# Four layers interleaved by superblocks, score tiles of 3 and 2 banks, TensorE in the listed order

One core of one Trainium2 chip runs the whole network. The metric is device time of one execution in microseconds (us). Two timed runs were slow, one of the kernel before beside e1 to e4 (610.69 us) and one of e8 (639.11); they stand in the medians, not in the ratios. A ratio is the mean time of one kernel's fast runs over that of the other's of the same rounds, so it is not quite the ratio of the medians that stand beside it. In the lines of the profile PE is TensorE, PEld its weight loads, DVE VectorE, ACT ScalarE, POOL GpSimd, SPq the queue from which most DMAs are issued. The granted clock (PEclk) is the share of full TensorE clock that the trace records: 1.0 is full, 0.5 half, and a mean over a stretch lies between.

## The reference

Four layers over x of 2048 rows and 512 columns: attention with a sliding window of 256 (32 heads of 16), linear attention, and both again with the same weights. Each adds to the residual.

```python
def _A_ref(x, wqkv, wo):                     # "attention" below
    q, k, v = split(x @ wqkv)                # 32 heads of 16
    scores = einsum("bhqd,bhkd->bhqk", q, k) * Dh ** -0.5
    mask = (i - j >= 0) & (i - j < 256)
    p = softmax(where(mask, scores, -1e9))
    return heads_joined(p @ v) @ wo

def _B_ref(x, wqkv, wo):                     # "the linear layer" below
    phi = lambda t: where(t > 0, t + 1, exp(t)) + 1e-6   # the "feature map"
    pq, pk = phi(q), phi(k)
    kv, z = sum_s(pk * v), sum_s(pk)         # over all 2048 rows
    o = (pq @ kv) / (pq @ z + 1e-6)
    return heads_joined(o) @ wo

x = A_x
x = x + _A_ref(_layernorm(x), A_wqkv, A_wo)
x = x + _B_ref(_layernorm(x), B_wqkv, B_wo)
x = x + _A_ref(_layernorm(x), A_wqkv, A_wo)
x = x + _B_ref(_layernorm(x), B_wqkv, B_wo)
```

(Condensed: batch 1, reshapes and transposes left out.) The sums kv and z are what limits interleaving: nothing of a linear layer's second half (numerator, denominator, output projection) can start before its last row block has been summed.

## The kernel before

The rows are treated in four *superblocks* of 512. For each, the attention layer makes q, k and v, then walks through score tiles: some small matmuls on 32 rows of the array fill a PSUM tile of three banks, ACT takes one exp over the tile, POOL zeroes what the mask forbids, and small matmuls multiply the result with v (P·V). The program lists side work (the next superblock's projections, the last one's output projection) evenly among the score tiles. A linear layer starts when the attention layer is done.

```python
psA = ctx_l.enter_context(tc.tile_pool(name="psA", bufs=2, space=PSUM))   # 2 score tiles of 3 banks
psM = ctx_l.enter_context(tc.tile_pool(name="psM", bufs=2, space=PSUM))   # all else, 1 bank each
# ...
            for gi, grp in enumerate(GROUPS):
                # ...
                for b, runs in enumerate(bins):
                    PTs.append(scores(I, grp, runs))
                    s += 1
                    if gi == 0 and b < len(lns):
                        lns[b]()                       # layernorm of the next superblock
                    if b >= 1 and steps:
                        steps.pop(0)()                 # P.V of the group before
                    while side and done < ((s - 4) * total) // (slots - 4):
                        side.pop(0)()                  # one projection
                        done += 1
# ...
        for li, lt in enumerate(layers):               # "ABAB", one after the other
            with ExitStack() as ctx_l:
                if lt == "A":
                    # ...
                    layer_A(xres, xres, wA, woA, a_idx)
                else:
                    layer_B(xres, xres, wB, woB, li == len(layers) - 1)
```

## Time and profile before

The median of the three runs timed first is 607.69 us (604.7 to 607.84); the profiled execution was a further, faster run of 602.24 us, with a span of 600.2 us. The stages, cut at the first and last exp of each attention layer:

| stage | us |
|---|---|
| head, to the first exp | 41.1 |
| first attention, four superblocks | 42.7, 43.0, 43.3, 41.1 |
| joint: linear layer, then the head of the second attention | 115.5 |
| second attention | 170.4 |
| tail: second linear layer | 103 |

One more view is TensorE's waits in the kernel before: who waited, for what, us in total, how often, and the longest.

```profile
PE O L318 <- POOL pt L308: 22.7, 35, 2.5
PE A L286 <- ACT pt L298: 14.6, 40, 0.9
PE py L490 <- DMA oT<-ob: 14.1, 13, 2.1
```

P·V (O) waits for masks, scores (A) for a score tile that ACT is still reading, and the linear layer's output projection (py) for a transposing DMA; each time 0.4 to 1.1 us on average.

### The profile page before, as it was taken

The numbers are of one execution on the slowest core, as the hardware profiler recorded it, in microseconds if no ns is written. First come the engines' busy times: TensorE is split into PE (matmuls) and PEld (weight loads), VectorE is DVE, ScalarE is ACT, GpSimd is POOL, SyncE is SP. The second block draws the span as 40 slices with busy tenths as digits, with TensorE's granted clock in tenths as the row PEclk, the third lists the DMA queues.
The fourth block names the chain that finished last, engine by engine and source line by source line (L and its number), as shares of the span: only waits on it lengthen the run. The fifth ranks groups of instructions, "written<-read, shape, count | busy, mean of one in ns | idle before, by whom it ended". The sixth has DMA issues, their size and how long they took to land. (4 is left out here: it accounts for less than half of the span.)

```text
span 600.2 us, 15126 instructions
## 1 busy us (share of the span) xinstructions
PE 460.0 (77%) x6032; PEld 250.1 (42%) x6114; DVE 332.5 (55%) x729; ACT 367.5 (61%) x373; POOL 272.1 (45%) x667
## 2 busy tenths in 40 slices
PE   0178888888878879995647788888887887899573
PEld 0133455545546534452213345554544553444231
DVE  7731546545623365777886154554562336677773
ACT  1557679799779824660025857988978892466000
POOL 9444457657556562200035435675755666320000
PEclk9996899999976678997988779899998788999787
DMA  9412115031020030211431211501302103021363
GB/s 302 127 27 60 16 37 75 2 48 30 2 64 11 3 80 10 41 31 35 72 70 36 57 19 34 78 2 42 35 2 53 24 2 76 14 44 29 74 120 92
DMA packets 83375, 29.66 MB, mean 49 GB/s; under 512 B 67936, under 2 KB 82784, under 8 KB 83296
## 3 DMA queue, kind: packets, MB, share of 16 engines
q1 hardware_dynamic: 78256, 23.88, 19.9%
q10 hardware_dynamic: 5040, 4.72, 2.6%
q8 instruction: 50, 0.82, 0.6%
q14 instruction: 29, 0.24, 0.1%
HBM read 6.29 MB, written 2.10 MB: 14 GB/s over the span
## 5 line engine op out<-in xcount | busy, mean ns | idle before, releaser
L298 ACT ACTIVATE pt<-A 128x1536 bf16<-128x1536 f32 (+1 forms) x228 | 281.0, 1321 | 52.9 <-PE A L286 46.3
L308 POOL TENSOR_SCALAR_AFFINE_SELECT pt<-pt 128x384 bf16<-128x384 bf16 (+3 forms) x456 | 184.3, 430 | 140.1 <-ACT pt L298 136.1
L318 PE MATMUL O<-vbd,pt 128*128 128x34 bf16 x2880 | 108.4, 182 | 27.7 <-POOL pt L308 22.7
L318 PEld LDWEIGHTS <-pt 128*128 128x128 bf16 x2880 | 89.8, 99 | 64.8 <-POOL pt L308 37.9
L286 PE MATMUL A<-qT,kb 32*128 32x192 bf16 (+3 forms) x1920 | 96.7, 249 | 17.1 <-ACT pt L298 14.6
L286 PEld LDWEIGHTS <-kb 32*128 32x128 bf16 x1920 | 50.1, 98 | 69.6 <-issue 64.3
L490 PE MATMUL py<-woB,oT 128*128 128x512 bf16 x124 | 39.3, 448 | 16.6 <-DMA oT<-ob 14.1
L327 DVE RECIPROCAL rall<-O 128x24 f32<-128x24 f32 (+1 forms) x48 | 13.8, 288 | 66.7 <-PE O L318 66.7
L164 POOL TENSOR_SCALAR ln_ve<-ln_mv 128x1 f32<-128x1 f32 x64 | 14.0, 225 | 69.7 <-DVE ln_mv L162 68.2
L221 PE MATMUL pq<-xnT,wA 128*128 128x512 bf16 x108 | 37.3, 432 | 9.2 <-DVE ln_stats L160 5.6
L271 PE MATMUL py<-woA,oT 128*128 128x512 bf16 x108 | 33.1, 397 | 14.1 <-DMA oT<-o_sb 12.4
L160 DVE BATCH_NORM_STATS2 ln_stats<-xres 128x6 f32<-128x512 f32 x64 | 42.5, 681 | 0.8
L235 DVE TENSOR_SCALAR kb<-pk,mask_even 128x512 bf16<-128x512 f32 x32 | 25.3, 791 | 28.6 <-PE pk L232 24.4
L232 PE MATMUL pk<-xnT,wA 128*128 128x512 bf16 x116 | 36.5, 414 | 5.0 <-ACT kb L237 2.5
L403 ACT ACTIVATE phi_e<-pkb 128x512 bf16<-128x512 f32 x32 | 19.1, 598 | 32.9 <-PE pkb L426 31.4
L166 POOL TENSOR_TENSOR ln_rstd<-ln_ve,mhalf 128x1 f32<-128x1 f32 x64 | 36.8, 582 | 4.3 <-ACT xn L178 0.4
L226 DVE CAST qT<-pq 128x512 bf16<-128x512 f32 x24 | 16.6, 691 | 33.5 <-PE pq L221 33.4
L432 PE MATMUL pvb<-wB,xnTb 128*128 128x512 bf16 x124 | 34.8, 395 | 0.2
L426 PE MATMUL pkb<-wB,xnTb 128*128 128x512 bf16 x122 | 34.0, 396 | 0.5 <-issue 0.4
L272 DVE TENSOR_TENSOR xres<-py,xres 128x512 f32<-128x512 f32 x32 | 22.0, 686 | 21.4 <-PE py L271 20.5
L245 PE MATMUL pv<-wA,xnT 128*128 128x512 bf16 x114 | 31.9, 380 | 2.2 <-ACT kb L237 0.8
L178 ACT ACTIVATE xn<-xres,ln_nmr,ln_rstd 128x512 bf16<-128x512 f32 x12 | 9.6, 827 | 37.9 <-DVE ln_nmr L176 37.9
(71 smaller groups left out, 522.0 us busy)
## 6 DMA issues: line engine op xcount, KB each, us to landing
vbd<-vst SPq DMA_DIRECT2D x128, 34.0 KB, 1.9
out_dram<-ost ACTq DMA_DIRECT2D x16, 128.0 KB, 1.9
wB<-in_B_wqkv_dram SPq DMA_DIRECT2D x1, 1536.0 KB, 11.2
xst<-in_A_x_dram SPq DMA_DIRECT2D x8, 128.0 KB, 2.6
wA<-in_A_wqkv_dram SPq DMA_DIRECT2D x2, 512.0 KB, 7.2
xst<-in_A_x_dram ACTq DMA_DIRECT2D x8, 128.0 KB, 4.0
wA<-in_A_wqkv_dram ACTq DMA_DIRECT2D x1, 512.0 KB, 4.3
woA<-in_A_wo_dram ACTq DMA_DIRECT2D x1, 512.0 KB, 8.2
```

The source lines that it names most:

```text
L160: nc.vector.bn_stats(stats[:], x_ap)
L166: nc.gpsimd.tensor_tensor(rstd[:], ve[:], mhalf[:], op=ALU.pow)
L221: nc.tensor.matmul(pq[:], lhsT=w[:, c, t * P:(t + 1) * P], rhs=xnTs[I][:, c, :], start=(c == 0), stop=(c == NCT - 1))
L232: nc.tensor.matmul(pk[:], lhsT=w[:, c, D + t * P:D + (t + 1) * P], rhs=xnTs[I][:, c, :], start=(c == 0), stop=(c == NCT - 1))
L271: nc.tensor.matmul(py[:], lhsT=oT[:, c, :], rhs=wo[:, c, :], start=(c == 0), stop=(c == NCT - 1))
L286: nc.tensor.matmul(A[:, g, r, pos:pos + n, :], lhsT=kbs[m // 8][32 * rg:32 * rg + 32, t, m % 8, :, :], rhs=qTs[I][32 * rg:32 * rg + 32, t, ...
L298: nc.scalar.activation(body[:, 0:2 * ng, 0:n, :], A[:, 0:ng, :, 0:n, :].rearrange("p g r s c -> p (g r) s c"), ACT.Exp, scale=0.25)
L308: nc.gpsimd.affine_select(out=v, in_=v, compare_op=ALU.is_ge, fill=0.0, base=1 if kind == 0 else -2, pattern=[[0, nx], [2 * s, 64]], chann ...
L318: nc.tensor.matmul(O[:, u, g, :, :], lhsT=PTs[b][:, s0:s0 + 2, :], rhs=vbd[(m // 8) % NV][:, m % 8, :, grp[g], :], start=(n == 0), stop=(n ...
L426: nc.tensor.matmul(pk[:], lhsT=xnT[:, c, u * P:(u + 1) * P], rhs=w[:, c, D:2 * D], start=(c == 0), stop=(c == NCT - 1))
L432: nc.tensor.matmul(pv[:], lhsT=xnT[:, c, u * P:(u + 1) * P], rhs=w[:, c, 2 * D:3 * D], start=(c == 0), stop=(c == NCT - 1))
L490: nc.tensor.matmul(py[:], lhsT=oT[:, c, :], rhs=wo[:, c, :], start=(c == 0), stop=(c == NCT - 1))
```

## The change

The intent: fill what attention leaves idle on TensorE and VectorE with the linear layer's work, and so take that work out of the joint and the tail. Most of a linear layer's first half (keys, values, their sums, queries) goes under the attention layer ahead of it, and half of its second half under the attention layer behind it. For that all layers share one set of pools. PSUM is divided anew: one score tile of three banks, one of two, and three single banks for everything else. Masks that come in pairs become a multiplication on VectorE. And TensorE gets its instructions in the order in which the program lists them; in the kernel before, the scheduler orders them.

```diff
-        psA = ctx_l.enter_context(tc.tile_pool(name="psA", bufs=2, space=PSUM))
-        psM = ctx_l.enter_context(tc.tile_pool(name="psM", bufs=2, space=PSUM))
+        ps3 = pool("ps3", 1, space=PSUM)
+        ps2 = pool("ps2", 1, space=PSUM)
+        psM = pool("psM", 3, space=PSUM)
+        vst = [fp.tile([P, 2, NP, VW], BF, name=f"vst{k}") for k in range(2)]   # was 3
 ...
+                        if len(ps) == 2 and y - x > 1:
+                            mt = tri[kind][:].unsqueeze(1).unsqueeze(1).to_broadcast([P, y - x, 2, 64])
+                            nc.vector.tensor_tensor(v, v, mt, op=ALU.mult)
+                            continue
 ...
+            for k, (size, units) in enumerate(phs):          # a phase is one score tile
+                scores(I, bins, size, units, where)
+                while due and due[0][0] <= k:
+                    due.pop(0)[1]()                          # P.V
+                    spent += .8
+                while items and items[0][1] <= k and (spent < total * (k + 1) / len(phs) or items[0][0] == 0):
+                    c, _, f = items.pop(0)                   # side work: (cost, first phase, what)
+                    f()
+                    spent += c
 ...
+        with tc.manual_schedule(engines={mybir.EngineType.PE}):
 ...
+                    prep = prep_items(I + 1, 5)              # q, k, v of the next superblock: from phase 5
+                    if I > 0:
+                        items += prep[:4] + outproj_items(I - 1, 0, 6) + prep[4:]
 ...
+                if I > 0:
+                    items += bkv_items(I - 1, 12) + bq_items(I - 1, 12)   # linear layer: from phase 12
```

(Cut to its core; the rest moves code, reads x without a cast, and renames.)

## The prediction

> **What bounds the kernel now.** I read the page first (busy shares, slices), then cut the trace at the first and last exp of each superblock (512 rows of an attention layer, four to a layer) and asked for busy time by stretch. The page's chain that ended last follows only the final two microseconds, so it does not name a bound.
>
> ```profile
> PE 460.0 (77%) x6032; PEld 250.1 (42%) x6114; DVE 332.5 (55%) x729; ACT 367.5 (61%) x373; POOL 272.1 (45%) x667
> PE   0178888888878879995647788888887887899573
> DVE  7731546545623365777886154554562336677773
> ACT  1557679799779824660025857988978892466000
> PEclk9996899999976678997988779899998788999787
> ```
>
> No engine is the bound for the whole span. The digits show alternation: ACT is high where VectorE is low (attention, slices 3 to 14 and 22 to 33), and ACT is near zero in slices 18 to 20 and at the end, where VectorE is high. The stages, columns being stretch, length, PE busy, PEld, DVE, ACT, POOL, granted clock, DMA share, GB/s:
>
> ```profile
> 0.00:41.10 41.10, 11.18 (x63) 5.12 (x65) 28.41 (x65) 15.19 (x24) 26.30 (x55) 1.00 0.54 166
> 41.10:83.80 42.70, 35.30 (x501) 18.97 (x510) 17.36 (x31) 31.17 (x30) 18.50 (x47) 0.84 0.16 32
> 126.80:170.10 43.30, 36.99 (x704) 21.82 (x709) 23.12 (x45) 37.15 (x30) 27.33 (x69) 1.00 0.16 29
> 170.10:211.20 41.10, 32.88 (x646) 21.31 (x649) 12.00 (x26) 37.00 (x30) 25.49 (x67) 0.66 0.10 23
> 211.20:270.00 58.80, 54.48 (x317) 26.76 (x323) 38.70 (x89) 27.62 (x47) 17.70 (x41) 0.92 0.20 41
> 270.00:326.70 56.70, 34.56 (x176) 14.45 (x178) 46.35 (x121) 8.60 (x14) 12.33 (x32) 0.85 0.30 56
> 557.00:600.20 43.20, 25.21 (x126) 11.25 (x128) 26.34 (x66) 0.00 (x0) 0.00 (x0) 0.80 0.45 99
> ```
>
> So the 600.2 us are: 41 of head, 170 of attention (four times about 42.5), 115.5 between the two attention layers (59 of the linear layer's projections and sums, near a TensorE bound, and 57 of its second half plus the next head, where VectorE leads), 170 of attention, 103 of tail. In attention ACT (37 of 43) and PE (37 of 43) are both close to full and wait for one another; VectorE is half idle there.
>
> ```profile
> L298 ACT ACTIVATE pt<-A 128x1536 bf16<-128x1536 f32 x144 | 198.7, 1488 | 21.3 <-PE A L286 17.4 <-POOL pt L308 3.8
> L298 ACT ACTIVATE pt<-A 128x1024 bf16<-128x1024 f32 x72 | 71.9, 1033 | 21.6 <-PE A L286 20.1 <-POOL pt L308 1.3
> L308 POOL TENSOR_SCALAR_AFFINE_SELECT pt<-pt 128x384 bf16<-128x384 bf16 x176 | 92.2, 540 | 60.6 <-ACT pt L298 58.8 <-PE O L318 0.8
> L308 POOL TENSOR_SCALAR_AFFINE_SELECT pt<-pt 128x192 bf16<-128x192 bf16 x128 | 43.8, 357 | 38.2 <-ACT pt L298 36.8 <-PE py L271 1.4
> L405 DVE SCALAR_TENSOR_TENSOR pks<-pkb,phi_e 128x512 bf16<-128x512 f32 x32 | 22.0, 689 | 3.0 <-DVE phi_e L404 0.5
> ```
>
> **What the Trainium skill says.** (1) "TensorE: Matmul & The Clock Gate", What's actually happening: the array falls to half clock after an idle window of about 3.4 us. The trace agrees in kind: the last superblock, with no projections beside its small matmuls, has a granted clock of 0.66 against 1.00 for the one before. (2) The same page, Step-by-step: only weight loads are pulled ahead, matmuls stay in program order. So what the program lists first blocks what follows if it waits; this trace cannot show it. (3) "VectorE: DVE Perf Modes", the perf-mode tier table: tensor_tensor runs at 2x on bf16 in SBUF, at 1x with PSUM; its fp32 add formula gives 691 ns for 512 columns, and the trace has 686 to 690. (4) "GPSIMD Engine Reference", Specifications: POOL's SBUF interfaces are shared with VectorE, with contention when VectorE has two SBUF inputs. The new mask multiplications are such; no run so far shows a price.
>
> **The change, part by part.**
>
> *Scores.* The packed tiles hold the same windows (40 per pair and superblock, 30 in the first). Counted from the two lists: score matmuls fall from 1920 to 1440 with the same columns; the P·V matmuls stay 2880. Exps become 16 of three banks and 16 of two per full superblock, against 20 and 10. Durations from the rows above: 16×1.488+16×1.033 = 40.3 us against 40.1; ACT gains nothing. PSUM goes from two 3-bank score tiles plus two others to one 3-bank, one 2-bank and three others.
>
> *Masks.* 456 selections on POOL (184 us) become 568 smaller ones plus 140 multiplications on VectorE. From the four POOL shapes (540, 416, 357, 294 ns at 384, 256, 192, 128 columns) I extrapolate 232 at 64: about 84 us per layer. The 140 on VectorE, estimated with the skill's fixed part at 2x as (192+151)/0.96 = 357 ns for the large form, are 48 us in all.
>
> *VectorE's total.* 332.5; minus casts of x (7), layernorm applications (14) and their small products (9), fewer small reciprocals and block-diagonal builds (14), vbd memset (4); plus 48 for masks, 22 for the 32 copies of v taken from ACT (690 ns), 14 for adding 32 partial sums (258 columns, estimated 0.43 us), 6 for copies no longer on ACT: about 375 to 410 us. POOL stays near 255 to 270 (48 us of layernorm applied at 0.81 replaces masks). ACT falls to about 325.
>
> *Interleaving.* Three quarters of the linear layer's first half goes under attention, and in the second attention half of the previous one's second half too. TensorE per full superblock, at full clock: 32 score tiles at about 0.23 (12 matmuls took 0.40 us, of which 0.18 latency) = 7.4; 384 P·V at 0.026 (24 took 0.77, same latency) = 10; projections (48+16+48 matmuls of 512 columns) at 0.216, the pace of the dense stretch at 240 to 270 us = 24; small ones 1: 42.5 us, and 47.5 with the second half of a linear layer. ACT: 37 of exp as measured plus 8 feature maps at 0.6 = 42. VectorE: keys 5.5, q and v 5.6, statistics 6.8, masks 6.8, P·V normalisation 4.8, residual 2.7, feature maps 8.0, v copies 2.8, sums 1.7 = 44.7, with the second half 51. All three stand at 42 to 51, where they were 37, 37 and 23.
>
> I take 90% for the fullest engine, hence 52 us for superblocks 2 and 3 of the first attention and 57 in the second; the last (no next projections: ACT 42 leads) 47; the first (ACT 31, half clock at its start) 35. Attention: 35+52+52+47 = 186, and 35+57+57+47 = 196; against 170 each.
>
> *Head.* x is loaded before the weights and read as bf16 without a cast, only four row blocks are normalised before the projections; the old kernel had 16 x-loads, all weights and 16 statistics there and projected from 30 to 41 us. Data at 5, normalised and transposed by 13, twelve projections on a partly cold array 15: 28 us, 13 less.
>
> *Between the layers.* PE is in program order here, so latencies add: P·V remainder 4.4; four transposes 6.3 (issue 1.3 each, 2.4 to landing), last projection and residual 1.6; layernorm to first transposed block 5.3; eight projections with waits for the sums 12; queries 3.5; second half of the first superblock 11 (denominator, four numerators, four transposes, projection); layernorm 9.3; next q, k, v 12 (VectorE-bound: 4×1.4+8×0.69); first score 1. Sum 66; 68 with some half clock; was 115.5.
>
> *Tail.* The first five items, 33, then four second halves at about 10, as each waits for its transposes before the next is issued: 74 with the store; was 103.
>
> Sum: 28+186+68+196+74 = 552. The runs of the old kernel lie 2 to 7 us above its profiled span, so about **555 us**.
>
> **The rivals.** *Program order stalls attention.* One matmul waiting for one of the three general PSUM banks holds all that follow, scores too. O keeps one bank nearly always; two serve some 28 projections per superblock. A feature-map bank is held about 0.95 for matmuls, 1.5 behind a running exp, 0.6, 0.3 and 0.7: 4 us. If that were every bank's hold, a superblock would need 28×4/2 = 56 us and more with VectorE's queue: superblocks of 60 to 65, total near 595. For it: ACT already lost 38 us to waits for scores with two equal tiles. Against it: copies of q and v hold a bank only about 2 us, and old attention ran well with one bank free beside O.
>
> *VectorE becomes the bound*, by the mask contention above and lumps: near 580; for it its digits rise from 23 to 45-51 in a superblock, against it POOL's load does not rise.
>
> *Overlap nearly perfect.* The dense 512-column work keeps the clock at 1.00 where it was 0.66 to 0.84, and full superblocks take 46 to 49: attention 170 and 178, mid 62, tail 65: near 508. For it: the clock row; against it: the latencies of program order.
>
> **Range and chances.** 80% from 508 to 600. Removed serial time (13+47+29 = 89 us) is surer than the price in attention (42 us). Faster by over 2% means under 595.5: 0.87; within 2%: 0.08; slower: 0.05.
>
> **What would show it.** First exp near 28 us instead of 41; superblocks of 50 to 58 with exps, feature maps and projections mixed, clock above 0.9 in the middle ones; VectorE's busy time 375 to 410; gaps of some 68 us between the last exp of one attention and the first of the next, and 74 after the last. Wrong would be: score matmuls mostly waiting for VectorE or for feature maps (first rival), a mask multiplication far above 360 ns (second), or a gap of 90 us and more between attentions, which would mean program order exposes latencies that the old scheduler had filled.

## The result, and the profile after

The changed kernel takes 673.08 us (670.99 to 673.85), against 607.03 for the kernel before in the same rounds: ratio 1.109 (1.105 to 1.113). It is slower by 11%, where faster by 9% was predicted, and outside the range. The page of the changed kernel, its busy times and slices:

```profile
PE 493.1 (74%) x5746; PEld 247.3 (37%) x5746; DVE 375.8 (56%) x833; ACT 324.7 (49%) x323; POOL 251.4 (38%) x727
PE   0669796989797598385566897999889759748573
DVE  4425266747464455476464457667856455547553
ACT  0256845794479368020041863677457937702000
PEclk9978788988898798797596858997899779879778
```

ACT and DVE have the busy times that the prediction gave them, and POOL nearly. But the ACT row no longer stands at 7 to 9 through the full superblocks: it swings between 4 and 9 within one. The windows by stage, with stretch, length, busy time of PE, PEld, DVE, ACT and POOL, granted clock, DMA share and GB/s:

```profile
0.00:37.20 37.20, 14.29 (x74) 7.08 (x75) 15.96 (x46) 6.89 (x12) 25.24 (x52) 1.00 0.66 198
142.80:207.30 64.50, 54.67 (x710) 27.52 (x707) 38.23 (x85) 41.76 (x41) 26.15 (x83) 0.87 0.12 27
207.30:265.30 58.00, 43.97 (x677) 24.37 (x674) 28.49 (x69) 41.02 (x41) 27.01 (x84) 0.84 0.11 20
265.30:343.70 78.40, 48.52 (x277) 21.05 (x274) 48.31 (x100) 4.81 (x10) 10.78 (x25) 0.77 0.18 35
457.40:524.30 66.90, 59.30 (x761) 29.89 (x758) 47.18 (x104) 42.24 (x42) 30.35 (x90) 0.90 0.21 42
581.70:668.90 87.20, 50.68 (x307) 22.53 (x304) 46.72 (x91) 4.81 (x9) 6.19 (x16) 0.79 0.25 62
```

The second line is a full superblock of the first attention: 64.5 us long, where ACT, the engine with the most to do before, is busy for 41.8. Stage by stage:

| stage | before | predicted | after |
|---|---|---|---|
| head | 41.1 | 28 | 37.2 |
| first attention | 170.1 | 186 | 228.1 |
| its superblocks | 42.7, 43.0, 43.3, 41.1 | 35, 52, 52, 47 | 42.0, 63.6, 64.5, 58.0 |
| joint | 115.5 | 68 | 78.4 |
| second attention | 170.4 | 196 | 238.0 |
| its superblocks | about 42.5 each | 35, 57, 57, 47 | 46.9, 66.8, 66.9, 57.4 |
| tail | 103 | 74 | 87.2 |
| span | 600.2 | 552 | 668.9 |

Head, joint and tail gave back 57 us, as intended though less than predicted (89). Attention lost 126, where 42 was predicted. So the question for the experiments is what makes a full superblock 64 to 67 us long, when ACT is busy for 42 us of it, VectorE for at most 47, and TensorE, by the prediction, needs 42.5 to 47.5.

Two readings of the trace gave the suspects. First a piece of the timeline of one full superblock: start, duration, engine, line, what, how many, and in brackets the idle time before it and what ended it.

```profile
159.17 1.04 ACT L301 ACTIVATE pt<-A 128x1024 bf16<-128x1024 f32 x1
159.70 2.97 PE L245 MATMUL py<-woA,oT 128*128 128x512 bf16 x13
162.51 1.03 PE L245 MATMUL pk<-xnT,wA 128*128 128x512 bf16 x4
163.37 1.03 PE L245 MATMUL pq<-xnT,wA 128*128 128x512 bf16 x4
164.33 0.39 PE L289 MATMUL A<-qT,kbd 32*128 32x320 bf16 x6
164.66 1.04 PE L245 MATMUL pk<-xnT,wA 128*128 128x512 bf16 x4
164.82 2.37 ACT L301 ACTIVATE pt<-A 128x1536 bf16<-128x1536 f32 x2 [4.61 <-issue]
170.03 0.39 PE L289 MATMUL A<-qT,kbd 32*128 32x192 bf16 x4
170.36 0.77 PE L341 MATMUL O<-vbd,pt 128*128 128x34 bf16 x24
171.06 0.40 PE L289 MATMUL A<-qT,kbd 32*128 32x64 bf16 x9
```

This is a **heap**. ACT finishes an exp at 160.21 and sits idle for 4.61 us, because TensorE has six projections, 24 matmuls of 512 columns, ahead of the next scores. (The view was asked for from 160 on and shows 13 of the first 16; a wider one has the first at 159.06.) The loop's running budget falls behind while the head of the item list may not run yet (nothing before phase 5, the output projections not before phase 9, and the rest of the projections behind them), and then pays out several items at once. The profile calls the wait "issue", but the exp starts half a microsecond after the score matmuls do. In the second attention the same gap reaches 9.6 us (407.94 to 417.52): in that heap the first key projection also waits 3.2 us for the layernorm's transposed block.

The same lines give TensorE's costs at full clock, from start to start. A projection takes 0.86 us ahead of another projection (162.51 to 163.37) but 0.96 ahead of scores (163.37 to 164.33). The score matmuls of a tile take 0.33 (164.33 to 164.66, 170.03 to 170.36), and a P·V step 0.70 (170.36 to 171.06). A full superblock has 32 score tiles, 16 P·V steps, 28 projections and some 1.4 us of sums: 32×0.33 + 16×0.70 + 28×0.90 + 1.4 = 48.4 us, where the prediction had 42.5. (Ahead of a projection a P·V step takes 0.62, from 158.44 to 159.06. With 0.62, 0.86 and 0.09 more for each of the 32 score tiles the sum is 48.8, so the 48.4 is an estimate to half a microsecond.)

Second, the staging tiles. The copy of v goes through a tile from which DMAs scatter it:

```profile
175.12 5.01 SPq L273 DMA_DIRECT2D vbd<-vst  x8
178.98 0.69 DVE L269 CAST vst<-pv 128x512 bf16<-128x512 f32 x1 [5.59 <-DMA vbd<-vst]
179.73 0.58 PE L245 MATMUL pkb<-wB,xnT 128*128 128x512 bf16 x1 [4.34 <-DVE vst L269]
```

There are two such tiles for four copies that now come close together. VectorE waits 5.59 us until the DMAs have left a tile; the projection that needs the PSUM bank which the copy holds waits behind it for 4.34; and all that is listed after that projection, scores too, waits with it. Over the whole trace the view of waits has:

```profile
DVE vst L269 <- DMA vbd<-vst: 19.0, 6, 5.6
PE pkb L245 <- DVE vst L269: 8.8, 2, 4.5
PE pkb L245 <- DMA xnT<-xn: 26.7, 4, 7.6
```

The last line is a wait for a layernorm's transposed block: 7.6 us in the joint, 7.6 in the tail, and 5.8 in the last superblock of each attention.

So the 64.5 us of the superblock are about 48.4 of TensorE at full clock, 6.3 more of busy time (54.67 less 48.4), which I put down to half clock, and 9.8 idle. The trace's clock records put it at half for 17.1 us of this superblock. Who makes whom wait is not shown by such a sum, hence the experiments.

### The profile page after: what moved, and what is told of

Its sections match the earlier page's. It is cut to its first block, busy times and chain, and to the rows that moved or that the text cites. A ratio compares the mean times of both kernels' runs of the same rounds, so it can differ in the third digit from the quotient of the medians.

```text
span 668.9 us, 14443 instructions
## 1 busy us (share of the span) xinstructions
PE 493.1 (74%) x5746; PEld 247.3 (37%) x5746; DVE 375.8 (56%) x833; ACT 324.7 (49%) x323; POOL 251.4 (38%) x727
## 5 line engine op out<-in xcount | busy, mean ns | idle before, releaser
L301 ACT ACTIVATE pt<-A 128x1536 bf16<-128x1536 f32 (+2 forms) x246 | 285.7, 1223 | 165.8 <-PE A L289 125.9
L324 POOL TENSOR_SCALAR_AFFINE_SELECT pt<-pt 128x128 bf16<-128x128 bf16 (+2 forms) x568 | 167.6, 324 | 210.2 <-ACT pt L301 208.2
L289 PE MATMUL A<-qT,kbd 32*128 32x320 bf16 (+4 forms) x1440 | 108.1, 279 | 40.6 <-ACT pt L301 39.9
L317 DVE TENSOR_TENSOR pt<-pt,tri 128x384 bf16<-128x384 bf16 (+1 forms) x140 | 51.1, 365 | 81.2 <-ACT pt L301 80.3
L289 PEld LDWEIGHTS <-kbd 32*128 32x128 bf16 x1440 | 43.5, 97 | 104.1 <-issue 96.0
L245 PE MATMUL pkb<-wB,xnT 128*128 128x512 bf16 x128 | 40.1, 443 | 35.6 <-DMA xnT<-xn 26.7
L245 PEld LDWEIGHTS <-oT 128*128 128x128 bf16 x256 | 27.6, 115 | 66.8 <-issue 23.3
L261 DVE TENSOR_TENSOR kbd<-pk,eo 128x512 bf16<-128x512 f32 x64 | 41.4, 682 | 17.1 <-PE pk L245 16.8
L219 POOL TENSOR_SCALAR xn<-xres,ln_nm,ln_rs 128x512 bf16<-128x512 f32 (+1 forms) x60 | 46.4, 786 | 3.1 <-DMA xnT<-xn 1.9
L212 DVE BATCH_NORM_STATS2 ln_st<-xres 128x6 f32<-128x512 f32 (+1 forms) x60 | 39.3, 678 | 9.4 <-DMA xres<-in_A_x_dram 9.1
L245 PEld LDWEIGHTS <-wA 128*128 128x128 bf16 x256 | 25.5, 108 | 46.4 <-issue 22.6
L245 PE MATMUL pvb<-wB,xnT 128*128 128x512 bf16 x128 | 39.2, 435 | 2.4 <-DVE vst L269 2.4
```

The lines of the kernel that those rows point to most:

```text
L212: nc.vector.bn_stats(st[:, u, :], xs[u])
L219: nc.gpsimd.tensor_scalar(xn[:], xs[u], nm[:, u:u + 1], rs[:, u:u + 1], op0=ALU.add, op1=ALU.mult)
L245: nc.tensor.matmul(ps[:], lhsT=lhs(c), rhs=rhs(c), start=(c == 0), stop=(c == NCT - 1))
L261: nc.vector.tensor_tensor(dst[:, t, :, :, :].rearrange("p m k h -> p (m k) h"), ps[:, hf * 256:(hf + 1) * 256].unsqueeze(2).to_broadcast([ ...
L289: nc.tensor.matmul(A[:, x, pos[x]:pos[x] + n, :], lhsT=kbd[half(m)][32 * rg:32 * rg + 32, t, m % 4, :, :], rhs=qTs[I][32 * rg:32 * rg + 32 ...
L301: nc.scalar.activation(body[:, x:y, 0:pos[x], :], A[:, x:y, 0:pos[x], :], ACT.Exp, scale=0.25)
```

## The experiments

The theories, in words: (a) TensorE's listed order lets one blocked instruction hold up scores; (b) the two staging tiles stall VectorE and TensorE behind it; (c) side work is listed in heaps, with stretches of none, so that TensorE and ACT take turns; (d) TensorE, at half clock or with more work than I counted, is simply full; (e) VectorE, through the new masks, is the bound. All lengths are those of the profiled execution. Superblocks are given from their first to their last exp, except in the windows and the stage table above, which run from a superblock's first exp to the first of the next; the two differ by up to 1.7 us.

### e1: the scheduler's order

```diff
-        with tc.manual_schedule(engines={mybir.EngineType.PE}):
+        with nullcontext():
```

> The changed kernel with one line undone: TensorE's instructions are put in order by the scheduler, as in the kernel before, instead of as listed. Theory 1 (the listed order is at fault: projections that were held back by their phase are listed in one heap of 4 to 6 us, scores come behind them and ACT starves): superblocks 2 and 3 fall from 64-67 us to 50-56, the whole from 673 to about 600. Rival (the interleaved load itself is too much for three general PSUM banks and VectorE, in whatever order): stays within 2% of 673.

Measured: 653.58 us against 604.13 before, ratio 1.081. Full superblocks became 60.0 and 59.5 in the first attention and 67.2 and 67.6 in the second. By the medians the listed order costs 20 us in this kernel (by the ratios 17, since the kernel before was 3 us faster on this chip), but with it undone 49 of the loss remain, which is between what the theory and the rival expected. Theory (a) is a part, not the whole cause.

### e2: four staging tiles

```diff
-        vst = [fp.tile([P, 2, NP, VW], BF, name=f"vst{k}") for k in range(2)]
+        vst = [fp.tile([P, 2, NP, VW], BF, name=f"vst{k}") for k in range(4)]
-            st = vst[nvst[0] % 2]
+            st = vst[nvst[0] % 4]
```

(A scratch tile of the final check was laid over a key buffer that is dead by then, to make room.)

> The changed kernel with four staging tiles for v instead of two (room made by placing one check tile over a key tile that is dead then). The trace shows six waits of VectorE for the DMA out of the staging tile, 19.0 us in all, the longest 5.6, with TensorE held behind it for about 4. Theory: these waits go, 10 to 19 us saved (about 655 to 663). Rival (they are slack that the next burst eats): under 5 us.

Measured: 651.43 us, ratio 1.077; 22 us less by the medians, 19 by the ratios. The same superblock as above:

```profile
135.60:193.10 57.50, 52.06 (x708) 27.13 (x704) 38.20 (x85) 41.79 (x41) 26.09 (x83) 0.91 0.14 30
```

64.5 became 57.5, TensorE's idle time in it fell from 9.8 to 5.4 us, and the clock rose from 0.87 to 0.91. Theory (b) holds, with some 20 us. Of the later kernels e4, e6 and e8 to e15 have the four tiles.

### e3 and e4: a cap on each phase

The first try at the heaps: each phase may list at most 1.1 times its even share of what is left. e3 has the two staging tiles, e4 four.

```diff
-                while items and items[0][1] <= k and (spent < total * (k + 1) / len(phs) or items[0][0] == 0):
+                left = sum(c for c, _, _ in items) + .8 * len(due)
+                cap, used = 1.1 * left / (len(phs) - k), 0.
+                while items and items[0][1] <= k and (used < cap or items[0][0] == 0):
                     c, _, f = items.pop(0)
                     f()
-                    spent += c
+                    used += c
```

> The changed kernel with the listed order kept, but each phase of attention may list at most 1.1 times its even share of the work still left, so that held-back work is spread over the phases to come and not caught up at once. Theory 1: the gaps of 4.4 to 5.4 us in ACT at those places go (two or three per superblock, some 10 us each superblock, 60 in all): about 615. Rival (the load, not its listing): within 2% of 673.

> Both of the two last edits together. If the two causes are separate, the savings add up: about 600. If the staging wait is only seen because of the heaps, it is no better than the even listing alone.

Measured: e3 701.82 us (ratio 1.162), e4 677.44 (1.122): **slower** by 29 and 26 than the same without the cap. Both miss what they were made to show. The edit has a flaw that I found in the trace afterwards: the share counts P·V steps and what is used does not, so work still ran out early. A window at the end of a superblock of e4:

```profile
130.00:142.00 12.00, 9.31 (x162) 5.85 (x162) 4.05 (x10) 11.29 (x11) 5.76 (x19) 0.68 0.01 1
```

For 12 us ACT is busy throughout (11.29), no projection is left to run beside it, and TensorE's clock falls to 0.68. That is the useful part of a failed experiment. The cap did remove the heaps from the full superblocks of the first attention: ACT's longest gap there is 2.4 us, where e2 has 4.7. Yet they are 4 us longer than in e2, with 17 us at half clock instead of 10. So the harm is not only in heaps, but in the stretches without side work. I did not test the cap again in repaired form by itself.

### e5: the interleaving alone undone

The linear layers' work goes back between the attention layers; tiles, masks, pools and listed order stay.

```diff
-                if I > 0:
-                    items += bkv_items(I - 1, 12) + bq_items(I - 1, 12)
                 attention(I, 0, items)
 ...
-            run(bkv_items(NSS - 1, 0))
-            kv_final()
-            run(bq_items(NSS - 1, 0))
+            layer_b1()          # all four superblocks of the linear layer's first half
```

> The changed kernel with the interleaving alone undone: the linear layer's projections and second half are listed after the attention layer; the 3- and 2-bank tiles, the masks on VectorE and the listed order stay. Theory (what moved under attention is what makes it long, the tiles and the order alone are harmless): full superblocks of 42 to 46 us instead of 57 to 67, but about 160 us between the attentions and 130 after, total 640 to 690. Rival (the tiles of 3 and 2 banks, or the listed order, cost attention itself): superblocks of 52 and more even so.

Measured: 667.21 us, ratio 1.102. A full superblock and the last one of the first attention:

```profile
132.40:180.10 47.70, 41.70 (x644) 22.41 (x641) 26.65 (x61) 37.43 (x33) 25.12 (x79) 0.86 0.16 35
180.10:223.20 43.10, 33.82 (x618) 21.05 (x617) 17.35 (x45) 37.00 (x33) 26.22 (x80) 0.62 0.13 28
```

The full superblocks are 48 (42 to 46 were expected), against 43 before and 64 to 67 with the interleaving: it costs 15 to 19 us in each, everything else in the change, the listed order included, about 5. The joint is 138 and the tail about 122, longer than before the change; that is my own plain placement of the linear layers as well as the listed order, so this kernel says nothing certain of joint and tail.

### e6: dummy projections to hold the clock

Four staging tiles, and wherever a phase lists less than one projection, a dummy projection whose result nobody reads (143 of them).

```diff
+        def warm():
+            proj("pw", lambda c: wA[:, c, 0:P], lambda c: wA[:, c, D:2 * D])
 ...
+                if ran < .8:
+                    warm()
```

> Four staging tiles, and in each phase that lists less than one projection a dummy projection of four 512-column matmuls, whose result nobody reads. [...] Theory (half clock costs some 4 us in each superblock): clock in attention above 0.95, total 10 to 30 us less than 651 although work is added. Rival (half clock falls where TensorE is not the limit): same as 651 or longer by the dummies.

Measured: 710.38 us, ratio 1.175: 59 slower than e2. The full superblock:

```profile
151.70:218.00 66.30, 64.25 (x776) 30.36 (x773) 38.14 (x85) 42.80 (x40) 26.27 (x83) 1.00 0.12 26
```

The clock is 1.00 and the superblock longer. The dummies' own time (143 at about 0.9 us, 130 us) is larger than anything that the clock could give back, so this kernel shows that filling the gaps with useless work doesn't pay, and nothing exact about the price of half clock (e2 is at half clock for 196 us in all). It does leave a check on the sum above: 68 matmuls more than in e2's superblock are 17 dummies, 15 us; 64.25 less that is about 49 us for a full superblock at full clock, near the 48.4.

### e7: the kernel before, in listed order

```diff
-        network(False)
+        with tc.manual_schedule(engines={mybir.EngineType.PE}):
+            network(False)
```

> The kernel before with one part of the change alone: its TensorE instructions issued as listed. Theory (listed order by itself is worth 20 us, as the run with the order left to the scheduler suggests, and exposes latency where layers join): 615 to 640. Rival (listed order is harmless, as the program of the kernel before is listed in pipeline order too): within 2% of 604.

Measured: 624.19 us, ratio 1.030. The listed order alone costs 17 us. TensorE's waits, to be held against those of the kernel before:

```profile
PE A L286 <- ACT pt L298: 39.9, 62, 1.4
PE py L490 <- DMA oT<-ob: 31.9, 18, 3.6
PE O L318 <- POOL pt L308: 8.1, 14, 1.2
```

Scores wait 39.9 us for their tile, where it was 14.6, and the output projection 31.9 for the transposes, where it was 14.1. Attention lost only some 2 us per layer; head (47.2 us) and joint (125.0) lost most. So the listed order alone, with full superblocks of 45 to 46 us, does not make them 64.

### e8, e14 and e11: the work listed evenly

e8 is four staging tiles and a new listing: layernorm one superblock ahead, so that projections may start from phase 2; part of the linear layer's work carried into the next superblock; and per phase an even share with a small credit.

```diff
-                while items and items[0][1] <= k and (spent < total * (k + 1) / len(phs) or items[0][0] == 0):
+                credit = min(credit + sum(c for c, _, _ in items) / (len(phs) - k), 1.8)
+                while items and items[0][1] <= k and (items[0][0] == 0 or credit >= .5 * items[0][0]):
                     c, _, f = items.pop(0)
                     f()
-                    spent += c
+                    credit -= c
 ...
-                    prep = prep_items(I + 1, 5)
+                    prep = prep_items(I + 1, 2) if I + 1 < NSS else []
+                    if I + 2 < NSS:
+                        items.append((0., 12, lambda I=I: lnA(I + 2, a)))
```

> Four staging tiles, and side work listed over the whole superblock: layernorm one superblock ahead so that projections may start in phase 2, query projections and half of the key and value ones of the linear layer carried into the next superblock's first phases, the second half of the linear layer started in the first superblock, each phase given its even share with a limit of two units. Theory 2 (the loss is that the first five phases and the last have no projections, so ACT bounds there and TensorE in the middle, at half clock at each border): full superblocks of 45 to 52 us, total 595 to 615, beside 651 for four staging tiles alone. Rival (interleaved work exceeds TensorE or the three general banks however it is spread): superblocks of 56 and more, 640 to 680.

Measured: 631.02 us, ratio 1.042, and a **wrong result** (relative error 0.45): the transposes of an attention output stood in a list whose head was held back, and ran after the next superblock had overwritten it. So its time settles nothing. e11 mends it: the transposes run at a fixed phase. In joint and tail e11 also lists the numerators of one superblock beside the output projections of the one before, and carried work beside the transposes. e14, made later, is e11 without the carried work and with joint and tail as in the changed kernel, so that each superblock of the first attention holds the same projections as in e2.

```diff
 e11, against e8
+                if k in timed:
+                    timed[k]()                       # phase 5: the transposes of the attention output
 ...
+                    for u in range(4):
+                        run(p[5 + u:6 + u])          # output projection of this superblock
+                        if nxt:
+                            run(nxt[1 + u:2 + u])    # numerator of the next
 e14, against e11
-                            now, carry = bkv[:4], bkv[4:] + bq
+                        now = bkv + bq
```

> The spread listing, mended (the output tile is transposed in phase 5, before the next group overwrites it, which made the run before wrong), and with the joints listed as a pipeline: the denominators and numerators of the next superblock beside the output projections of the one before, and the carried projections in the waits for transposes. Theory: attention as in the wrong run (about 195 and 212 us) or less, 62 instead of 78 to 86 us between the attentions, 66 instead of 82 to 87 after: 575 to 600, correct. Rival (the joints are bound by other latencies): 615 or more.

> Listed order, four staging tiles, layernorm a superblock ahead so that projections start in phase 2, even shares, but nothing carried from one superblock to the next and the joints as in the change. Theory 2: most of the saving in attention comes from filling the first phases, so full superblocks of 49 to 54 in the first attention, total 595 to 620. Rival (the carried work was what helped): superblocks of 56 to 58, 640 to 650.

Measured: e11 582.07 us, correct, ratio 0.963 (0.958 to 0.968); e14 608.88 us, correct, ratio 1.007. TensorE is in listed order in both. The two full superblocks of the first attention in e14:

```profile
76.10:127.10 51.00, 49.15 (x689) 24.63 (x695) 39.98 (x92) 42.08 (x42) 30.15 (x91) 1.00 0.27 48
127.10:183.50 56.40, 50.54 (x704) 25.95 (x709) 38.24 (x85) 42.34 (x42) 26.42 (x85) 0.94 0.15 31
```

With the same 28 projections in each they take 50.5 and 55.7 us from first to last exp, against 56.8 and 57.8 in e2, and in the first the clock is 1.00 with TensorE busy for 49.2: again near the 48.4. Both attentions together are 42 us shorter than in e2 (402 against 444), which is the whole difference of the two kernels. Theory (c) holds: this much of the loss lay in how the work was listed, not in how much there was.

e14 holds a sharper comparison within one kernel. In its first full superblock projections start after 2 us; in the second the output projections, which may not run before phase 9, stand at the head of the list and hold back the rest. The first 11.6 us of each:

```profile
76.10:87.70 11.60, 11.55 (x184) 5.94 (x183) 8.99 (x19) 10.55 (x10) 6.02 (x21) 1.00 0.39 66
127.10:138.70 11.60, 8.31 (x194) 5.68 (x192) 4.71 (x14) 11.37 (x11) 6.82 (x22) 0.74 0.24 48
```

In the second ACT sets the pace, TensorE does small matmuls alone and loses clock, and that superblock ends 5.4 us longer (56.4 against 51.0) with the same projections. It is hardly shorter than in e2 (57.5), although its layernorm was early too: an early layernorm helps only if the list then uses it.

In e11 a full superblock of the first attention has 24 projections, since part of the linear layer's are handed to the next superblock, and from the last superblocks eight to the joint and eight to the tail. Its window, and in the next fence TensorE's only wait in it:

```profile
126.50:175.80 49.30, 46.07 (x680) 22.88 (x679) 33.92 (x76) 40.62 (x39) 26.90 (x83) 0.97 0.16 35
```

```profile
PE A L289 <- ACT pt L301: 3.2, 5, 1.0
```

Attention is 17 us shorter than in e14, and joint and tail are not longer for the handed-on work but shorter, 75.9 and 77.4 against 78.1 and 86.4: it runs where TensorE waited. How much is due to the carrying and how much to the pairing was not separated. The 62 and 66 us that the expectation gave for joint and tail were not reached.

### e9: less work for TensorE

Four staging tiles and the old listing: the linear layers' projections contract two of four chunks, 5.2 us less TensorE work per full superblock. Its output is wrong, which doesn't matter for the time.

```diff
-            for c in range(NCT):
+            nk = NCT // 2 if name in ("pkb", "pvb", "pqb") else NCT
+            for c in range(nk):
```

> Four staging tiles, and each of the linear layer's query, key and value projections contracts over two of four chunks (a wrong result, on purpose): 2 of 4 matmuls go, everything that reads the banks stays. Theory 3 (TensorE's own time bounds the full superblocks: 52 us busy of 57.5 in the run with four staging tiles): twelve projections lose two matmuls of 0.216 us each, 5.2 us, and full superblocks fall from 57-58 to about 52-53 in the first attention, the total by 40 or so (48 projections per layer, some in the joints) to about 615. Rival (the three general banks, VectorE or ACT bound them): superblocks within 1.5 us of before.

Measured: 641.11 us, ratio 1.060. The full superblocks of the first attention are 55.9 and 56.2, against 56.8 and 57.8 in e2: 1.3 us less on average, not 5.2. The mean clock fell from 0.851 to 0.802, and from e2 to e9 TensorE's busy time in these superblocks fell by 2.6 us on average, so part of what was taken away seems to have come back as half clock. TensorE's sum of work was not the bound in the old listing. The rival (the three general PSUM banks, VectorE or ACT) expected this small gain; e10 speaks against VectorE's masks, and e14, with the same three banks and the same projections, against the banks.

### e10: the masks back on POOL

Four staging tiles, no mask multiplications on VectorE.

```diff
-                        ps = [q for q in (left[0], left[0] + 3) if q in left]
+                        ps = [q for q in (left[0], left[0] + 3) if q in left][:1 if y - x > 1 else 2]
```

> Four staging tiles, and the 140 mask multiplications of VectorE given back to POOL as selections of one window each (51 us of VectorE's time go; POOL gets 280 more selections of about 0.42 us, 100 us or more). Theory 3 (TensorE bounds): within 2% of 651, or a little longer by POOL's delay ahead of the value matmuls. Rival (VectorE's load or its contention with POOL bounds): at least 2% faster.

Measured: 653.43 us, ratio 1.080, full superblocks of 58.2: hardly a change from e2, although VectorE is busy for 335 us in all instead of 375. Theory (e) falls. One detail is worth having. POOL's selections of 192 columns in the changed kernel, VectorE's mask multiplications there, and the same selections in e10:

```profile
L324 POOL TENSOR_SCALAR_AFFINE_SELECT pt<-pt 128x192 bf16<-128x192 bf16 x180 | 73.5, 425 | 117.4 <-ACT pt L301 117.4
L317 DVE TENSOR_TENSOR pt<-pt,tri 128x384 bf16<-128x384 bf16 x110 | 41.3, 376 | 74.8 <-ACT pt L301 74.0 <-POOL ln_rs L214 0.2
```

```profile
L324 POOL TENSOR_SCALAR_AFFINE_SELECT pt<-pt 128x192 bf16<-128x192 bf16 x400 | 129.5, 357 | 93.2 <-ACT pt L301 92.8
```

With multiplications running on VectorE a selection takes 425 ns on average, without 357, as in the kernel before. The changed kernel's own trace says why: of its 180 such selections the 96 that overlap a mask multiplication by more than 50 ns take 537 ns in the median, the 84 others 352. POOL is busy for 38% of the span, and e10 is no faster, so it costs nothing here.

### e12, e13 and e15: the order again, and how far it goes

e12 is e11 in the scheduler's order. e13 is e2 in the scheduler's order, with the old listing. e15 is e12 with all of x loaded ahead of the second layer's weights.

```diff
 e12, e13
-        with tc.manual_schedule(engines={mybir.EngineType.PE}):
+        with nullcontext():
 e15
             load_x(1)
+            load_x(2)
+            load_x(3)
             load_rest()
```

> The same program with TensorE's order left to the scheduler. The listed order alone cost the kernel before 17 us and the changed one 20. Theory (in a program that is listed evenly nothing is left to gain): within 2% of the run with the listed order. Rival (the scheduler fills waits that a list cannot foresee): 10 to 20 us faster.

> Four staging tiles and the scheduler's order, work items as in the change. Theory 2 (the items' phases leave the first phases without projections; no order of TensorE mends that alone): the two savings of 20 and 22 us add at best, 625 to 635, superblocks of 52 and more. Rival (the even listing was not needed, only the ring and the order): 600 or less.

> The fastest version so far (563 us) with all loads of x ahead of the three later weights. In its trace VectorE stands still from 15.5 to 21.3 us for a block of x that lies behind 2.5 MB of weights, and the first normalised block comes at 22.9. Theory: first exp at about 33 instead of 40, 555 to 558. Rival (the scheduler moves another wait there): within 1%.

| kernel | us | ratio to before | full superblocks, first attention | second |
|---|---|---|---|---|
| changed | 673.08 | 1.109 | 63.7, 64.7 | 67.0, 67.0 |
| e2: + four staging tiles | 651.43 | 1.077 | 56.8, 57.8 | 63.7, 65.2 |
| e14: + even listing, layernorm ahead | 608.88 | 1.007 | 50.5, 55.7 | 59.9, 56.0 |
| e11: + carried work, paired second halves | 582.07 | 0.963 | 47.6, 48.7 | 56.5, 57.9 |
| e12: + scheduler's order | 562.96 | 0.931 | 46.4, 46.3 | 54.1, 55.8 |
| e15: + x first | 557.45 | 0.923 | 46.5, 46.3 | 54.1, 55.7 |
| e13: e2 + scheduler's order | 637.44 | 1.053 | 53.4, 54.4 | 65.3, 64.7 |

(In e14, e11, e12 and e15 one second half of a linear layer has moved to the first superblock of the second attention; in e11, e12 and e15 the superblocks hold fewer projections, as told.) e12 is 19 us faster than e11, as its rival had it. e13 shows that the scheduler's order does not repair a bad listing: it gives 14 us there, and 74 us lie between e13 and e12. The windows of e15 for a full superblock of each attention and, between them, the joint:

```profile
116.40:163.10 46.70, 44.73 (x668) 22.84 (x677) 32.78 (x76) 40.69 (x38) 26.44 (x82) 1.00 0.17 37
207.90:283.20 75.30, 54.22 (x352) 25.32 (x356) 57.33 (x123) 8.36 (x14) 15.09 (x33) 0.89 0.20 44
319.80:374.20 54.40, 47.72 (x685) 24.06 (x692) 37.71 (x87) 39.20 (x35) 28.99 (x84) 0.94 0.25 56
```

In the first, TensorE is busy for 44.7 of 46.7 us at full clock: there it is the bound. One stretch of the bad kind is left: key and value projections that are handed on keep their phase, 17, within a layer. In the third superblock of the second attention of e11 no projection starts for 19.5 us (396.1 to 415.6), and it is the longest of that kernel, 59.6 us to the next first exp; in e15 it is 57.4. Mending it was not tried. e15 is the fastest version, 7.7% under the kernel before and 17% under the changed one.

## Why the prediction was wrong

The span was predicted at 552 us and is 668.9, a miss of 117. By stages: the four full superblocks 44, the two first ones 19, the two last ones 21, the head 9, the joint 10, the tail 13.

**The step that failed** is "I take 90% for the fullest engine, hence 52 us for superblocks 2 and 3". It divides an average load by a utilisation, and so presumes that side work lies evenly beside the exps. (Nor does 52 follow: the fullest engine there was VectorE with 44.7, and 44.7/0.9 is 49.7; the 57 does follow from 51.) The change lists it from phases 5, 6, 9 and 12 on. Ahead of those ACT sets the pace and TensorE falls to half clock (142.8 to 149.0: ACT busy 5.3 of 6.2 us, clock 0.59); behind them TensorE works off a heap with ACT idle for 4 to 5 us at a time. Such a superblock took 64 to 67 us. With the same work per superblock listed evenly, still in listed order, and with enough staging tiles, the first attention took 36.7, 50.5, 55.7 and 49.9 us in e14, close to the predicted 35, 52, 52 and 47. That closeness is luck in part: the 50.5 is some 48.4 us of TensorE nearly full, not 44.7 at 90%. So the prediction was one for another listing than the one in the diff. The phases stood there as plain numbers; I summed the items and did not lay them out in time.

**A wait that was not looked for.** The prediction never mentions the staging tiles, which went from three to two while the copies came closer together: some 20 us by e2.

**A mis-sized term.** "TensorE per full superblock, at full clock: ... 42.5 us" is 48.4 by start-to-start times: scores 0.33 per tile instead of 0.23, and about 0.1 more for a P·V step (0.70 instead of 0.62) or a projection (0.96 instead of 0.86) that has scores behind it. I had subtracted a latency from the duration of a group; the distance between the starts of two groups is the cost. Busy time was 54.7; half clock would account for the 6 more. This term did not decide the result in the changed kernel (e9), but with fewer projections it is what bounds the full superblocks of e15: 32×0.33 + 16×0.70 + 24×0.90 = 43.4, where 44.7 were measured.

**Head, joint and tail.** The direction was right, the sizes were not. In the head, the statistics of a later x block, whose load lay behind the weights on the same DMA queue, stood ahead of the first normalisation in VectorE's order (which the scheduler makes in every kernel here), and the prediction had that normalisation done by 13 us:

```profile
19.90 1.29 DVE L212 BATCH_NORM_STATS2 ln_st<-xres 128x6 f32<-128x512 bf16 x2 [5.54 <-DMA xres<-in_A_x_dram]
21.52 1.46 DVE L235 TENSOR_SCALAR xn<-xres,lf_mv,lf_rs 128x512 bf16<-128x512 bf16 x4
```

e15 tests it: with x loaded first the head is 34.0 us, against 40.2 in e12. In the joint (68 predicted, 78.4 measured) TensorE's waits are:

```profile
PE pkb L245 <- DMA xnT<-xn: 7.6, 1, 7.6
PE py L245 <- DMA oT<-ob: 6.7, 2, 4.7
PE pn L449 <- DVE ob L452: 6.6, 2, 5.3
PE py L245 <- DMA oT<-o_sb: 3.0, 1, 3.0
```

For the first I had 5.3. The second and third, 13.3 together, are numerators and output projections of one superblock in turn, each exposing VectorE's or a transpose's latency; the prediction had 11 us for one second half and laid the other wholly beside a layernorm. e15 brings the joint only to 75.3, with eight more projections in it.

**The rivals.** *Program order stalls attention* gave superblocks of 60 to 65 us, which is about what came (its total, near 595, was not); but by every general bank held too long, which the trace doesn't show. The bank that it does show held is the one behind the staging tile, and undoing the order gave 20 of the 117 us. So its number was right for a reason that was mostly not the one. *VectorE becomes the bound* falls by e10. *Overlap nearly perfect*, 508, is not reached by anything tried; the nearest is 557, whose full superblocks of 46.5 in the first attention (with 24 projections in place of 28) are those of this rival, while those of the second, the joint and the tail (54 to 56, 75 and 74) are not.

**What was right:** 1440 score and 2880 P·V matmuls, VectorE at 375.8 us (375 to 410), ACT at 324.7 (325), POOL at 251.4 (255 to 270, just missed), a mask multiplication of 376 ns (357; the add formula behind this estimate stands in the cited page's section on the TRN2 errata, not in its tier table). Counting work was reliable. Placing it was not.

**What stays open:** the price of half clock by itself (e6 is buried under its dummies, and e9 lowers the clock while it removes work), whether a repaired cap of the kind of e3 would help without the earlier layernorm, and what the late projections of the third superblock still cost e15.

## What to carry to other kernels

When work is moved under another stage, lay it out phase by phase before believing a utilisation: an engine that is idle on average may have no work allowed when it is idle and too much when it is not. Then look at the smallest ring of buffers on the path of what now comes closer together, since in listed order one full ring stops everything behind it. And leave the order of instructions to the scheduler unless the listing is better than its own: here the listed order cost 17 us in the old kernel, 20 in the changed one, 14 with four staging tiles and 19 in the mended one.

## What the Trainium skill lacked or had wrong

- "TensorE: Matmul & The Clock Gate", What's actually happening, ties half clock to an idle window. Here the granted clock fell to 0.62 in a stretch in which the profile, which models the ends of matmuls, has TensorE busy for 33.8 of 43.1 us (e5, last superblock of the first attention), and to 0.66 with 32.9 of 41.1 in the kernel before. Both stretches hold small matmuls with four projections beside them (the prediction's first point says none). A later section of the page, on a second failure mode, has the clock swing when TensorE idles briefly and often, without a length. What the page's activity monitor counts as busy is not shown by these runs.
- "TensorEngine Tiling (Array Packing)", Key Properties, says that changing the tiling mode drains TensorE, without a size. A projection ahead of 32-row score matmuls took 0.96 us from start to start, ahead of another projection 0.86; a P·V step 0.70 and 0.62: about 0.1 us per change, if the drain is what makes the difference.
- "GPSIMD Engine Reference", Specifications, names contention with VectorE instructions that have two SBUF inputs, without a size. The runs agree with it: 425 against 357 ns for a selection of 192 columns with and without mask multiplications on VectorE, and 537 against 352 in the median for those that overlap one and those that don't.
- No page that I found gives a price for issuing TensorE's instructions in the listed order; four pairs of runs here show 14 to 20 us of some 600.
